# A decode step of attention and MLP layers: the last 64 outputs computed once, q spread by copies, and w4 in longer runs

## The chip, the core and the metric

The kernel runs on one core of one Trainium2 chip. The metric is the device time in microseconds of one execution; the time shown is the median of several runs. One further execution was recorded by the hardware profiler, and the page and the trace quoted here are of that one. PE is the matrix engine (PEld its weight loads), DVE the vector engine, ACT the scalar engine, POOL GpSimd, SP the engine whose queue issues the loads.

## What is computed

Eight sequences (B = 8) with one new token each, D = 448 features, go through an attention layer, an MLP layer, and both again with the same weights and the same K and V caches:

```python
x = A_x
x = x + A(layernorm(x))     # pass 0
x = x + B(layernorm(x))
x = x + A(layernorm(x))     # pass 1
x = x + B(layernorm(x))

def A(x):                   # 16 query heads, 8 K/V heads, 4096 cached keys, 256 wide
    q = x @ wq                                  # 448 -> 4096
    p = softmax(q . k_cache / 16)               # each K/V head serves two query heads
    return (p . v_cache) @ wo                   # 4096 -> 448

def B(x):                   # S = 1: the shifted branch through w1, w2 is zero
    x1 = x + 0
    return x1 + gelu(layernorm(x1) @ w3) @ w4   # 448 -> 1792 -> 448
```

With one token a sequence, each shifted part of B's first branch is padding, so w1 and w2 are not used. All inputs are bf16. A layer's caches are 268 MB, and pass 1 needs the same caches after pass 0, so nearly all of the traffic is K and V.

## The kernel before, in words

**Loads.** K and V come in pieces of 1 MB (two K/V heads, a quarter of the keys), each into one of 15 places in SBUF (`places`, L73). `emit_loads` (L616) issues them on SP's queue in the order of use, as soon as a place is free; eight DMA semaphores go round, so a load also waits for the one eight before it. Eleven pieces of each sequence stay in their places from pass 0 to pass 1, and a twelfth is parked in PSUM (`away`, L677) and brought back (`back`, L684). While they stay, few places are left to go round.

**Order.** `tasks` (L518) lists (pass, sequence, pair of K/V heads) by hand; each task has four K items and four V items, the V items one task later (L545). For a K item the vector engine transposes the place in two instructions (`transpose_k`, L640), PE multiplies by q (`scores`, L647), and after two items ACT takes the exponentials (L669). For a V item PE multiplies by the probabilities (`pv`, L708; in the last sequence `pv_cols`, L725). The place is then free, and the next load goes out.

**Chains.** What comes between attention and the next projection is written as generators: `first_half` and `chain` for pass 0 (wo, the MLP, the q of pass 1), `last` and `first_last` for pass 1, `rest` for the MLP of the first four sequences together. `step` (L768) lets each advance a little at each item, paced by the total number of its steps that `add_gen` is given. So their products stand between scores and PV products in PE's program, and their vector work between K transposes. The last MLP of the other four sequences runs at the end, after all loads (L899 onwards).

**The 448 features** are kept as columns: three groups of 128 partitions and one of 64 (`xT`, L169). In `wq` and `w3` the rows of the last 64 features are split over the partitions: half of the output columns in partitions 0 to 63, the other half in 64 to 127 (`split_tile`, `load_split`, L156 to L163). The input of those products, `xb`, therefore needs the last 64 features in the lower half for some products and the upper half for others (`wblk`, L174), with zeros in the other half. To have them in both, `xT` holds the last 64 features twice, and all that adds to xT makes them twice: `rows_to_cols` (L194) and `add_cols` (L332, five groups, of which fc 3 and fc 4 are the same 64 columns of the weights into the two halves). The weights of the mean, `wv` (L138), count each half by 0.5.

**Spreading q.** Scores need q in a block form `qbd` with zeros elsewhere. `spread_q` (L299) copies the selected rows of q to all four groups of 32 partitions by 16 products, and four `tensor_scalar` instructions with the 0/1 columns of `quad` write the whole of qbd. In pass 0 q comes from `qT1`, laid out with the eight sequences innermost, so one sequence's 32 columns are 16 bytes apart; in pass 1 from `qT2`, contiguous. Each (pass, sequence) is spread once (L807) into one of three buffers.

**w4** is loaded by L752 with hidden unit 128 c + p in partition p, block c: runs of 896 bytes. `mlp_hidden` (L352) makes the hidden units in the same order, 14 blocks of 128, each from 128 neighbouring columns of w3.

Of the kernel before, what the change touches and what calls it, by code (L numbers as in the profile page):

```python
# [17 lines left out]
def kernel(  # L18
# [39 lines left out]
    HC = F // 128  # L58
    scale_exp = float(Dh) ** -0.5
# [21 lines left out]
    def scratch(a, n):  # L81
# [8 lines left out]
    quad = consts.tile([128, 4], FP32, name="quad")  # L90
    nc.vector.tensor_reduce(
        quad[:], ident.rearrange("p (a j) -> p a j", a=4), mybir.AxisListType.X, ALU.add
    )


# [26 lines left out]
    for t in [sc] + o_banks:  # L122
        nc.vector.memset(t[:], 0.0)
# [14 lines left out]
    nc.vector.memset(wv[:, 3:4], 0.5 / D)  # L138
# [29 lines left out]
    w4_sb = consts.tile([128, HC, D], BF16, name="w4_sb")  # L168
    xT = consts.tile([128, 4, Bn], FP32, name="xT")  # L169
# [4 lines left out]
    def wblk(t, cols, c, fc):  # L174

        if fc < 3:
            return t[:, fc * cols + 128 * c : fc * cols + 128 * c + 128], fc
        half = cols // 2
        if 128 * c < half:
            return t[:, 3 * cols + 128 * c : 3 * cols + 128 * c + 128], 3  # L180
        return t[:, 3 * cols + 128 * c - half : 3 * cols + 128 * c - half + 128], 4

    def rows_to_cols(row, nb):

        idn = identb[:nb, :nb]
        ps = room_ps("y", nb)[:, 0 : 4 * nb].rearrange("p (f b) -> p f b", b=nb)
        for fc in range(3):  # L190
            nc.tensor.matmul(
                ps[:, fc, :], row[:nb, 128 * fc : 128 * fc + 128], idn, start=True, stop=True
            )
        for r in range(2):  # L194
            nc.tensor.matmul(
                ps[64 * r : 64 * r + 64, 3, :], row[:nb, 384:448], idn, start=True, stop=True
            )
        return ps

    def norm(x, nb, twice):  # L200
# [57 lines left out]
        parts = ((slice(0, 128), 0, 3, 0), (slice(0, 64), 3, 4, 3), (slice(64, 128), 3, 4, 4))  # L258
        for pp, f0, f1, to in parts:
            dst = xbs(nb)[pp, to : to + f1 - f0, :]  # L260
            if nb == 1:
                nc.vector.tensor_scalar(dst, xc[pp, f0:f1], rl[pp], c, ALU.mult, ALU.mult)  # L262
            else:
                nc.vector.scalar_tensor_tensor(
                    dst,
                    xc[pp, f0:f1],
                    c,
                    rl[pp].unsqueeze(1).to_broadcast([pp.stop - pp.start, f1 - f0, nb]),
                    ALU.mult,
                    ALU.mult,  # L270
                )
# [7 lines left out]
    def project_q(b0, nb, qT):  # L279
# [3 lines left out]
        for j in range(2):  # L283
            for h in range(Hq):
                for fc in range(4):
                    w, xi = wblk(wq_sb, HD, 2 * h + j, fc)
                    nc.tensor.matmul(  # L287
                        q_ps[:, j * Hq + h, :],
                        w,
                        xbs(nb)[:, xi, :],  # L290
                        start=(fc == 0),
                        stop=(fc == 3),
                    )
                if h % 4 == 3:
                    yield
# [3 lines left out]
    def spread_q(qT, qbd):  # L299


        qs = misc[:, 128 : 128 + 4 * NB2].rearrange("p (e n) -> p e n", e=4)
        for ep in range(4):
            e2, par = ep // 2, ep % 2
            sel = identb[:, 64 * e2 : 64 * e2 + 64].rearrange("p (j r) -> p r j", r=2)[:, par, :]
            for a in range(4):
                nc.tensor.matmul(  # L307
                    qs[32 * a : 32 * a + 32, ep, :], sel, qT, start=True, stop=True
                )
        yield  # L310
        for a in range(4):
            u = a // 2
            nc.vector.tensor_scalar_mul(  # L313
                qbd[:, :, :, a, :],
                qs.rearrange("p e (f g u h) -> p (e f) u g h", f=2, u=2, h=2)[:, :, u],
                quad[:, a : a + 1],
# [13 lines left out]
    def add_cols(y_ps, rhs, w, rows, every, open=None):  # L330

        for fc in range(5):  # L332
            lo, hi = (128 * fc, 128 * fc + 128) if fc < 3 else (384, 448)
            r = y_ps[:, fc, :] if fc < 3 else y_ps[64 * (fc - 3) : 64 * (fc - 2), 3, :]
# [14 lines left out]
            if fc % every == every - 1 or fc == 4:  # L349
                yield  # L350

    def mlp_hidden(b0, nb):  # L352
# [3 lines left out]
        for c in range(HC):  # L356
            for fc in range(4):
                w, xi = wblk(w3_sb, F, c, fc)
# [386 lines left out]
    nc.vector.tensor_copy(xT[:], ps0)  # L745
# [6 lines left out]
    nc.sync.dma_start(w4_sb[:], B_w4.rearrange("(c p) d -> p c d", p=128))  # L752
# [36 lines left out]
    for idx, it in enumerate(items):  # L789
        n, kv, c = it  # L790
        ps, b, gp = tasks[n]
        if (ps, b, gp, kv, c) == (0, Bn - 1, REST, 0, 0):
            assert pairs_done[1, MID - 1] == 4
            add_gen("rest", 0, rest(), idx + 1, idx + 18, 25)
# [4 lines left out]
        if kv == 0:  # L799
# [7 lines left out]
            if "q" not in st:  # L807
                qbd = work.tile([128, 8, GP, 4, 2], BF16, tag="qbd", bufs=3)
                run(spread_q(st["qT"][:] if ps == 1 else qT1[:, :, b], qbd))
                st["q"] = qbd  # L810
# [12 lines left out]
            if not paired(n, c):  # L823
                scores(p, c, st["q"], gp, between=turn)
            elif c % 2 != ps:
# [4 lines left out]
                if abs(two[1] - two[0]) == 1:  # L830
                    scores(two[0], x, st["q"], gp, also=two[1], between=turn)
                else:
                    scores(two[0], x, st["q"], gp, between=turn)
                    scores(two[1], x + 1, st["q"], gp)
# [8 lines left out]
        else:  # L843
# [6 lines left out]
            if final and gp in free:  # L850
                pv_cols(oc, slot, c, gp)
                if c % 2 == 1:
# [10 lines left out]
                            5,  # L863
# [14 lines left out]
            if c == 3:  # L878
                done = pairs_done[ps, b] = pairs_done.get((ps, b), 0) + 1
                if done == 2 and ps == 0:  # L880
                    add_gen("chain", b, first_half(b, st), idx + 1, idx + 21, 14)
                elif done == 2:
                    add_gen("chain" if final else "last", b, first_last(b, st), idx + 1, idx + 13, 11)
                elif done == 4 and ps == 0:
                    add_gen("chain", b, chain(b, st), idx + 1, first_of[(1, b), 0] - 1, 43)
# [15 lines left out]
    nc.vector.tensor_add(xs, xs, st["y"])  # L901
# [65 lines left out]
```

The softmax here doesn't subtract the row's maximum and nothing guards it: scores larger than these inputs give would overflow.

## Time and profile before

| | |
|---|---|
| median of 7 runs | 1119.17 us (1117.76 to 1121.62) |
| the profiled execution | 1116.47 us |
| its span | 1114.7 us |
| granted PE clock, mean | 0.586 of full speed |
| K loads, 1 MB each, median from issue to landing | 200, 11.6 us |
| V loads, 1 MB each, median from issue to landing | 216, 10.0 us |
| DVE K transposes (L645), two a load | 400, 469.0 us busy |
| PE scores (L660) | 7072 products, 268.0 us busy |
| PE PV products (L716) | 1984 products, 245.9 us busy |
| PE products with wo and w4, one sequence at a time, 64 wide (L341) | 512 and 224, 193 and 194 ns each |
| PEld weight loads of w3 (L359) | 560, 105 ns each |
| DVE writes of qbd (L313) | 64, 277 ns each |

The page divides the span into 40 slices. The busy digits are tenths, PEclk the clock that PE was granted in tenths, GB/s what the DMA engines moved:

```profile
PE   3135668657864688536894378944787478877866
...
DVE  5145554656365545555375553655537453585372
...
PEclk9999555755565555665555555555555555565575
DMA  9999999999999999999999999999999999999994
GB/s 357 383 421 421 412 395 417 419 407 416 405 422 421 404 405 421 418 422 381 398 420 421 421 390 399 418 421 410 398 400 421 417 403 413 419 380 412 405 419 175
```

A slice is 27.9 us. The rate is 412 to 422 GB/s in some, and 380 to 407 in others; the first two and the last one are lower still. In the groups of the page, busy time is the union of overlapping instructions, and the time of one matmul includes its way through the array, so products that follow each other start closer together than their duration says. Where spacings of starts are given below, they are read from the trace's instruction records, and sizes and durations of single DMA packets from its packet records.

### The profile page before, as it was taken

The numbers are of one execution on the slowest core, as the hardware profiler recorded it, in microseconds if no ns is written. First come the engines' busy times: TensorE is split into PE (matmuls) and PEld (weight loads), VectorE is DVE, ScalarE is ACT, GpSimd is POOL, SyncE is SP. The second block draws the span as 40 slices with busy tenths as digits, with TensorE's granted clock in tenths as the row PEclk, the third lists the DMA queues.
The fourth block names the chain that finished last, engine by engine and source line by source line (L and its number), as shares of the span: only waits on it lengthen the run. The fifth ranks groups of instructions, "written<-read, shape, count | busy, mean of one in ns | idle before, by whom it ended". The sixth has DMA issues, their size and how long they took to land.

```text
span 1114.7 us, 31093 instructions
## 1 busy us (share of the span) xinstructions
PE 734.9 (66%) x14193; PEld 459.4 (41%) x14193; DVE 595.2 (53%) x1040; ACT 135.9 (12%) x393; POOL 15.6 (1%) x25
## 2 busy tenths in 40 slices
PE   3135668657864688536894378944787478877866
PEld 2013445334541455214552145522554244645555
DVE  5145554656365545555375553655537453585372
ACT  0001101110110011101020011200111111111110
POOL 0000000000000000000000000000000000000000
PEclk9999555755565555665555555555555555565575
DMA  9999999999999999999999999999999999999994
GB/s 357 383 421 421 412 395 417 419 407 416 405 422 421 404 405 421 418 422 381 398 420 421 421 390 399 418 421 410 398 400 421 417 403 413 419 380 412 405 419 175
DMA packets 65170, 448.78 MB, mean 403 GB/s; under 512 B 6920, under 2 KB 10896, under 8 KB 11408
## 3 DMA queue, kind: packets, MB, share of 16 engines
q1 hardware_dynamic: 65008, 446.80, 98.3%
q8 instruction: 111, 1.82, 0.6%
q14 instruction: 19, 0.16, 0.0%
q10 hardware_dynamic: 32, 0.00, 0.0%
HBM read 446.77 MB, written 0.01 MB: 401 GB/s over the span
## 4 chain that ended last, share of the span: by engine, by line
DMA 59%; PE 20%; DVE 14%; SPq 3%; issue 2%; ACT 1%; POOL 0%; POOLq 0%; DVEq 0%; ACTq 0%
DMA places<-in_A_k_cache_dram 53%; DVE places L645 10%; PE sc L660 8%; DMA places<-in_A_v_cache_dram 5%; PE o L716 5%; PE misc L341 3%; PE misc L447 2%; SPq L161 2%; SPq L637 1%; DVE qbd L313 1%; DMA wq_sb<-in_A_wq_dram 1%; PE misc L287 1%; ACT p_n L669 0%; PE store L341 0%; PE store L730 0%
## 5 line engine op out<-in xcount | busy, mean ns | idle before, releaser
L645 DVE STREAM_TRANSPOSE places<-places 128x1024 uint32<-128x1024 uint32 x400 | 469.0, 1218 | 256.9 <-DMA places<-in_A_k_cache_dram 255.5
L660 PE MATMUL sc<-places,qbd 128*8 128x128 bf16 (+1 forms) x7072 | 268.0, 308 | 245.8 <-DVE places L645 215.4
L660 PEld LDWEIGHTS <-qbd 128*8 128x8 bf16 x7072 | 169.8, 107 | 347.3 <-issue 169.7
L716 PE MATMUL o<-places,ptw 128*16 128x512 bf16 x1984 | 245.9, 595 | 73.8 <-DMA places<-in_A_v_cache_dram 71.1
L669 ACT ACTIVATE p_n<-sc 128x256 bf16<-128x256 f32 x128 | 95.6, 747 | 738.2 <-PE sc L660 738.2
L341 PEld LDWEIGHTS <-wo_sb 128*128 128x128 bf16 (+1 forms) x1600 | 64.8, 125 | 43.4 <-issue 43.1
L716 PEld LDWEIGHTS <-ptw 128*16 128x16 bf16 x1984 | 44.2, 103 | 89.7 <-issue 80.9
L447 PEld LDWEIGHTS misc<-R,o_sb 128*128 128x128 f32 x248 | 54.6, 305 | 30.3 <-issue 19.5
L447 PE MATMUL misc<-R,o_sb 128*128 128x8 f32 x248 | 59.9, 352 | 10.6 <-ACT o_sb L442 4.9
L341 PE MATMUL misc<-OT,wo_sb 128*128 128x1 bf16 (+1 forms) x1280 | 56.7, 177 | 1.0 <-DVE qbd L313 1.0
L287 PEld LDWEIGHTS <-wq_sb 128*128 128x128 bf16 x1152 | 36.0, 104 | 45.6 <-issue 40.0
L287 PE MATMUL misc<-xb,wq_sb 128*128 128x1 bf16 x1024 | 34.7, 166 | 9.2 <-DVE xb L262 6.0
L669 ACT ACTIVATION_READ_ACCUMULATOR p_n<-sc 128x1 f32 x128 | 34.0, 266 | 0.0
L296 DVE CAST qT<-misc 128x32 bf16<-128x32 f32 x8 | 1.5, 191 | 59.5 <-PE misc L287 59.5
L703 ACT CAST ptw<-misc 128x128 bf16<-128x128 f32 x64 | 17.5, 274 | 128.0 <-PE misc L696 105.0
L442 ACT COPY o_sb<-o 128x256 f32<-128x256 f32 x62 | 23.5, 379 | 72.0 <-PE misc L447 63.8
L341 PEld LDWEIGHTS <-w_sb 128*128 128x128 bf16 (+1 forms) x630 | 25.9, 124 | 14.9 <-issue 14.8
L245 POOL TENSOR_TENSOR t<-t,nhalf 128x2 f32<-128x2 f32 (+2 forms) x18 | 13.3, 739 | 1085.4 <-DVE t L252 986.5
L313 DVE TENSOR_SCALAR qbd<-misc,quad 128x64 bf16<-128x64 f32 x64 | 13.7, 277 | 26.4 <-PE misc L307 26.4
L687 DVE STREAM_TRANSPOSE places<-store 128x512 uint32<-128x512 uint32 x32 | 20.1, 684 | 11.2 <-PE sc L660 11.2
L341 PE MATMUL misc<-HT_t,w_sb 128*128 128x1 bf16 (+1 forms) x560 | 25.2, 177 | 0.2 <-DVE HT_t L382 0.2
L359 PEld LDWEIGHTS <-w_sb 128*128 128x128 bf16 x560 | 18.0, 105 | 16.3 <-issue 16.0
(95 smaller groups left out, 267.8 us busy)
## 6 DMA issues: line engine op xcount, KB each, us to landing
places<-in_A_v_cache_dram SPq DMA_DIRECT2D x216, 1024.0 KB, 10.0
places<-in_A_k_cache_dram SPq DMA_DIRECT2D x200, 1024.0 KB, 11.6
wo_sb<-in_A_wo_dram SPq DMA_DIRECT2D x1, 3584.0 KB, 25.7
wq_sb<-in_A_wq_dram SPq DMA_DIRECT2D x3, 1024.0 KB, 7.0
w_sb<-in_B_w_dram SPq DMA_DIRECT2D x1, 1568.0 KB, 15.9
w_sb<-in_B_w_dram SPq DMA_DIRECT2D x3, 448.0 KB, 25.6
wq_sb<-in_A_wq_dram SPq DMA_DIRECT2D x2, 256.0 KB, 10.1
w_sb<-in_B_w_dram SPq DMA_DIRECT2D x2, 112.0 KB
```

The lines of the kernel that those rows point to most:

```text
L161: nc.sync.dma_start(t[:, fc * cols : (fc + 1) * cols], src[fc * 128 : fc * 128 + 128, :])
L287: nc.tensor.matmul(q_ps[:, j * Hq + h, :], w, xbs(nb)[:, xi, :], start=(fc == 0), stop=(fc == 3),)
L313: nc.vector.tensor_scalar_mul(qbd[:, :, :, a, :], qs.rearrange("p e (f g u h) -> p (e f) u g h", f=2, u=2, h=2)[:, :, u], quad[:, a : a + 1],)
L341: nc.tensor.matmul(r, w[:, i, lo:hi], rhs(i), start=start, stop=stop, skip_group_check=open is not None,)
L359: nc.tensor.matmul(h_ps[:, c * nb : c * nb + nb], w, xbs(nb)[:, xi, :], start=(fc == 0), stop=(fc == 3),)
L442: nc.scalar.copy(o_sb[:], o_ps[:, Dh * n : Dh * n + Dh])
L447: nc.tensor.matmul(ot_ps[:, n, j], o_sb[:].rearrange("p (i j) -> p j i", j=2)[:, j], R[:, n], start=True, stop=True,)
L645: nc.vector.transpose(w, w)
L660: nc.tensor.matmul(sc[32 * k : 32 * k + 8, 128 * x : 128 * (x + nx)], qbd[:, ep, gp].rearrange("p a h -> p (a h)"), v, start=(n == 0), sto ...
L669: nc.scalar.activation(p_sb[:, :, :, 2 * u : 2 * u + 2].rearrange("p t i x -> p x t i"), sc[:, 256 * u : 256 * u + 256].rearrange("p (x t ...
L687: nc.vector.transpose(slot[:].bitcast(U32)[:, 512 * n : 512 * n + 512], store[n][:].bitcast(U32))
L716: nc.tensor.matmul(o_ps[32 * q : 32 * q + 16, :].rearrange("p (i d) -> p i d", i=2), ptz[:, at : at + 16], rows[:, q, i : i + 2], start=(b ...
```

## The change

- **wo and w4, 64 outputs once.** `add_cols` has four groups instead of five; the fourth writes the last 64 features to partitions 0 to 63 only. `xT` keeps them there once, with zeros in the upper half; `rows_to_cols` makes them once, and `wv` has 1/D in the lower half and 0 in the upper. `norm` writes the upper copy in `xb` from the lower half of xc (an instruction whose input and output lie in different partitions). The misc bank is zeroed at the start.
- **q spread once.** `spread_q` makes four products instead of 16, into 32 partitions, and four copies that read these 32 partitions and write one group of 32 each. The zeros of qbd are written once at the start, so the buffers are two constants (`qbds`) instead of three rotating ones. When a (pass, sequence) is needed that is in neither, the one whose next use is farthest is replaced and spread again later: 18 spreads instead of 16. `quad` goes.
- **w4 in runs of 6,272 bytes.** Hidden unit 896 s + 7 p + c is in partition p, block 7 s + c. `mlp_hidden` makes its blocks in that order, so each takes every seventh column of w3 (`wblk` has a step). The products are the same in number and size.
- Totals given to `add_gen` follow the steps that went: 25 to 23, 14 to 13, 43 to 41.
- At the end, the addition to xT (L901) is in two instructions, of 128 and of 64 partitions, as is the first copy into xT.

The order of loads on SP is as before, but for the shape of w4's.

```diff
-    nc.vector.memset(wv[:, 3:4], 0.5 / D)
+    nc.vector.memset(wv[0:64, 3:4], 1.0 / D)
+    nc.vector.memset(wv[64:128, 3:4], 0.0)
...
+    qbds = [consts.tile([128, 8, GP, 4, 2], BF16, name=f"qbd{k}") for k in range(2)]
+    for t in qbds:
+        nc.vector.memset(t[:].rearrange("p n g a h -> p (n g a h)"), 0.0)
+    q_of = [None] * len(qbds)
...
-    def wblk(t, cols, c, fc):
+    def wblk(t, cols, at, step, fc):
...
+        s2 = at // half
+        lo = fc * cols + (at if fc < 3 else at - s2 * half)
+        return t[:, lo : lo + 127 * step + 1 : step], fc if fc < 3 else 3 + s2
...
-        qs = misc[:, 128 : 128 + 4 * NB2].rearrange("p (e n) -> p e n", e=4)
+        qs = misc[0:32, 128 : 128 + 4 * NB2].rearrange("p (e n) -> p e n", e=4)
         for ep in range(4):
...
-            for a in range(4):
-                nc.tensor.matmul(
-                    qs[32 * a : 32 * a + 32, ep, :], sel, qT, start=True, stop=True
-                )
+            nc.tensor.matmul(qs[:, ep, :], sel, qT, start=True, stop=True)
         yield
         for a in range(4):
             u = a // 2
-            nc.vector.tensor_scalar_mul(
-                qbd[:, :, :, a, :],
+            nc.vector.tensor_copy(
+                qbd[32 * a : 32 * a + 32, :, :, a, :],
                 qs.rearrange("p e (f g u h) -> p (e f) u g h", f=2, u=2, h=2)[:, :, u],
-                quad[:, a : a + 1],
             )
...
-        for fc in range(5):
-            lo, hi = (128 * fc, 128 * fc + 128) if fc < 3 else (384, 448)
-            r = y_ps[:, fc, :] if fc < 3 else y_ps[64 * (fc - 3) : 64 * (fc - 2), 3, :]
+        for fc in range(4):
+            lo, hi = 128 * fc, min(128 * fc + 128, D)
+            r = y_ps[0 : hi - lo, fc, :]
...
-                w, xi = wblk(w3_sb, F, c, fc)
+                w, xi = wblk(w3_sb, F, F // 2 * (c // H2) + c % H2, H2, fc)
...
-    nc.sync.dma_start(w4_sb[:], B_w4.rearrange("(c p) d -> p c d", p=128))
+    nc.sync.dma_start(
+        w4_sb[:].rearrange("p (s c) d -> p s (c d)", s=2),
+        B_w4.rearrange("(s p c) d -> p s (c d)", s=2, p=128),
+    )
...
-            if "q" not in st:
-                qbd = work.tile([128, 8, GP, 4, 2], BF16, tag="qbd", bufs=3)
-                run(spread_q(st["qT"][:] if ps == 1 else qT1[:, :, b], qbd))
-                st["q"] = qbd
+            if (ps, b) not in q_of:
+
+                def next_use(k):
+                    return next((m for m in range(n, len(tasks)) if tasks[m][:2] == q_of[k]), 999)
+
+                k = max(range(len(qbds)), key=next_use)
+                q_of[k] = (ps, b)
+                run(spread_q(st["qT"][:] if ps == 1 else qT1[:, :, b], qbds[k]))
+            qbd = qbds[q_of.index((ps, b))]
...
-    nc.vector.tensor_add(xs, xs, st["y"])
+    nc.vector.tensor_add(xs[:, 0:3], xs[:, 0:3], st["y"][:, 0:3])
+    nc.vector.tensor_add(xs[0:64, 3], xs[0:64, 3], st["y"][0:64, 3])
```

## The prediction

> **What bounds the kernel now.** I read the busy rows and queues of the page first, then the rate of the DMA over time, then, load by load from the trace, when each 1 MB load was issued and when it landed.
>
> ```profile
> PE 734.9 (66%) x14193; PEld 459.4 (41%) x14193; DVE 595.2 (53%) x1040; ACT 135.9 (12%) x393; POOL 15.6 (1%) x25
> ...
> q1 hardware_dynamic: 65008, 446.80, 98.3%
> q8 instruction: 111, 1.82, 0.6%
> ...
> DMA 59%; PE 20%; DVE 14%; SPq 3%; issue 2%; ACT 1%; POOL 0%; POOLq 0%; DVEq 0%; ACTq 0%
> ```
>
> The DMA engines hold packets 98.3% of the time and the chain of waits is mostly DMA. In full flow one load lands 2.48 us after another (423 GB/s); 446.8 MB at that pace is 1057 us, so 58 us of the 1114.7 us span are elsewhere. By 10 us windows held against 421 GB/s: 6.8 us before 50 us, about 25 us in dips between 130 and 1050 us, some 22 us at the end, mostly the 14 us after the last V load (1100.4 us).
>
> The dips matter most for a change to PE. They lie where the places not kept are few and two K and two V loads circulate. There a K transpose starts 0.02 us after its load lands almost every time: the engines wait for the DMA. A load lands either 2.48 us after the one before or, issued late, some 6.85 us after issue. I compared each landing with the later of those two. From 100 to 1062 us, 176 loads with an instruction packet (16,384 B) in flight came late by 29.4 us in all; 195 without one by 3.6 us. So the dips are mainly instruction fetches, each worth 0.27 us (29.4 / 111, which credits them with all of it). Late issue, which PE can cause, accounts for some 12 us and overlaps this.
>
> **The change, part by part.** All sums are against the profiled execution (1116.47 us: span 1114.7 plus 1.8); the median shown is 1119.17, 2.7 us more, and I put the difference on the median.
>
> **w4 in 6,272 B runs.** The load issued at L752 has 1,792 packets of 896 B and gets 256 of 6,272 B.
>
> ```profile
> GB/s 413 419 419 426 361 379 377 377 383 378 380 387 403 406 358 220 330 292 340 390 416 436 419 426 419 419 419 419 419 433 419 426 419 400 433 419 426 419 419 419
> ```
>
> This is the DMA rate from 20 to 70 us, 1.25 us a figure: 358, 220, 330, 292, 340 at 37.5 to 43.75 us is where w4 and the end of w3 pass. By packets: 1,792 x 51.8 ns / 16 engines is 5.8 us; between 3,584 B (150 ns) and 8,192 B (319 ns) a 6,272 B packet comes to 249 ns, and 256 of them to 4.0 us: 1.8 us gained. By landings: w4 came 4.45 us after the load before it, where 1.6 MB needs 3.8: 0.6 us gained. I take **-1.5**, nearer to the packets because the slow slices also hold the end of w3. A rule speaks against it: the Trainium skill, "DMA: Bandwidth & Descriptors", Specifications, puts full line rate at 512 B and more, which would make this 0. The trace has 17 B/ns for 896 B and 26 for 8,192 B, so the row decides. Nothing else hides or eats it: from 47 to 128 us every load lands on the 2.48 us pace, so all later landings move with it.
>
> **Fewer instructions.** PE's program falls from 27,768 to 26,508 rows; a fetch of 16,384 B holds 256 of 64 B, so 4.9 fewer fetches, at 0.27 us: **-1.3** (between 0 and that).
>
> **One 64-wide group instead of two.** `add_cols` had fc 3 and 4 of 64 columns each, the second a copy for the lower partitions.
>
> ```profile
> L341 PEld LDWEIGHTS <-wo_sb x32: 128/157/158, 518.0 to 519.4; 128*64 128x64 bf16 x32
> ...
>   DVE xT L479: 2.3, 1
> ```
>
> Those 32 loads start 48 ns apart, groups with one tile position 55 ns, while 128-wide ones start 27 ns apart. 446 go: 256 for wo one batch at a time, 112 for w4, 64 for wo with four columns, 14 for w4 with four: some 23 us of PE. Most of it lies beside DMA. It counts where the vector engine stands at L479 until the group is done, and the next K waits: the K transposes after these groups began 0.36, 0.62, 0.04, 0.38, 0.20, 0.61, 0.57 and 0.51 us after landing, 3.3 us in all. The group shrinks by 0.7 us, so this wait goes, but the load two later was late by only part of it: **-1.5** (0 to -3.3). What is late next is the K load itself.
>
> **w3 read at a step of 7.** This is the price of the w4 layout: hidden unit 7p + c belongs to partition p, so each of the 560 w3 weight loads at L359 takes columns 14 B apart.
>
> ```profile
> L359 PEld LDWEIGHTS <-w_sb x56: 103/104/114, 525.6 to 530.3; 128*128 128x128 bf16 x56
> ...
> L307 PE MATMUL misc<-qT,identb x16: 230/242/255, 503.7 to 503.9; 128*32 128x32 bf16 x16
> ...
> L307 PE MATMUL misc<-qT,identb x16: 187/188/235, 556.7 to 556.9; 128*32 128x32 bf16 x16
> ```
>
> The first row is contiguous; its loads start 26.7 ns apart. The other two are the same `spread_q` product: in pass 0 its 32 columns lie 16 B apart, in pass 1 2 B. Matmul ends are modelled, so I use starts: rounds of four tiles begin 51 to 59 ns apart in pass 0 and 27 in pass 1. Four streams that take a new 16 B line at each step run 2.1 times slower. The V products at L730 load weights at a 4 B step and keep 27 ns. Two rules meet here. The Trainium skill, "TensorE: Matmul & The Clock Gate", Weight-path perf modes, allows the fast load of 128 columns any step up to 1,024 elements: no cost. "SBUF — State Buffer", in its note on cachelines (16 B), wants two hits a line, yet calls 8 bf16 a free stride; the pass 0 row is exactly 8 and pays, while 14 B steps get 8 columns from 7 lines. I take the row: 27 to 56 ns, +29 ns a load. Lower bound 0; upper bound one line after another, 112 lines in 93 ns at the 0.83 ns pace of a fast load, or more.
>
> Where it lies: eight chains of 56 loads get +1.6 us each in steps of at most 16 or 24 loads (+0.5 to +0.7). Behind a step wait the PV products, whose V load is issued after them, and L377 on the vector engine with the next K. In the chain at 525 us, PE then idles 1.15 us for the K transpose and L377 ends 0.57 us before the next K lands, so most is covered: **+0.5** over the run. The `rest` stretch (950 to 995 us) has PE nearly full; 46 narrow loads go there (-2.4 us), 56 strided ones come (+1.6): **-0.5**.
>
> **Spreading q.** 16 products in four tile columns (about 0.14 to 0.20 us first to last start) become 4 in one, which no longer overlap: 4 x 27 or 4 x 56 ns, no gain. L313's four instructions of 277 ns (0.86 us) become four copies of 32 partitions and 64 columns; the nearest cast from PSUM is L296 at 191 ns for 32 columns, so 0.7 to 0.9 us: 0. The copies overwrite a buffer whose last scores stand before the products in PE's order, so two buffers for three add no wait. But 18 spreads replace 16: batch 2 of pass 0 and batch 5 of pass 1 are spread again, each about 1.2 us of PE and DVE in turn; the first falls in a PE stretch with the DMA at full rate, the second near 1000 us: **+0.5**.
>
> **Start.** Three more memsets (misc 0.49 us as its neighbours at L123, two of half L114's size) and a second xT copy lie before 12.6 us, while the q products wait for wq: 0. If exposed, below 1 us.
>
> **Tail.** DMA sets its start at 1100.4 us. What PE saves before (fc 4 of batch 7's wo, 0.9 us) is hidden by that V load; only the last group shrinks, 4 x 55 ns: -0.2. L901 becomes two: +0.16. Then
>
> ```profile
> 1107.21 1.65 PE misc L359 x56
> ```
>
> stands bare on the chain: 56 x 29 ns: +1.64. **+1.6** in all.
>
> **Pacing.** Generators lose one or two of their steps and totals fall with them; SP's order is the same but for w4. I count 0.
>
> **Sum:** -1.5 - 1.3 - 1.5 + 0.5 - 0.5 + 0.5 + 1.6 = **-2.2**, so 1114.3 against 1116.47, and 1119.17 - 2.2 = **1117.0**. What can be told from no change is 0.2%, 2.2 us: the forecast stands on that edge.
>
> **Rivals.** *A, slower: the strided load goes line by line.* At 93 ns a load is +66: tail +3.7 where the forecast has +1.6; each step of 16 or 24 becomes 1.1 to 1.6 us longer, past the 0.6 to 1.2 us of cover, about 1.3 us for each of eight chains (+10). With the gains kept: +9, **1128**, and far more if a line costs two steps. For it: four streams ask for 3.5 lines a step, L730 only one. Against: pass 0's spread asks for four lines a step and paid 2.1 times. It decides from about 70 ns a load. *B: no penalty.* Tail 0, middle -1.3 more: -5, **1114**. For it: L730 and the mode rule; against: the spread rows. *C: the middle hides everything.* The load behind each wait was late by little, and fetches may not be the cause: -1.5 + 0.5 + 0.5 + 1.6 = +1, **1120**.
>
> **How the numbers follow.** Forecast 0.54 (own range 1113 to 1121: faster 0.30, same 0.17, slower 0.07), A 0.26 (slower), B 0.13 (faster), C 0.07 (same 0.05, slower 0.02). Faster 0.43, same 0.22, slower 0.35. The range runs from 1112, below B, to 1129, A at 93 ns; beyond lies A at a heavier price.
>
> **What would show it.** Weight loads of the w3 line 53 to 60 ns apart and about 3.3 us for the 56 in the tail (1.65: B; over 5: A). w4 landing about 1.5 us earlier and the first loads after it too. Some 106 instruction packets of 16 KB. K transposes at once after landing where L479 had kept them. I am wrong if w3's steps move V issues or K transposes by a microsecond, or if the new order of steps sets other loads late.

## The result, and the profile after

The changed kernel takes **1129.69 us** (median of 12 runs, 1124.67 to 1135.46); the kernel before took 1119.18 beside it (30 runs). The ratio is 1.0087, with a 95% interval of 1.0070 to 1.0103: some 10 us slower, where 1117.0 was forecast. The granted PE clock is no cause: the eight executions at 0.58 to 0.59 of full speed took 1129.5 us in the mean, the four at 0.62 to 0.63 took 1128.7. The profiled execution took 1127.6 us, with a span of 1125.8, against 1116.47 and 1114.7.

The busy rows, the queues and the chain by engine, from the page of the changed kernel:

```profile
PE 722.8 (64%) x13562; PEld 450.2 (40%) x13562; DVE 600.3 (53%) x1054; ACT 136.5 (12%) x393; POOL 15.6 (1%) x25
...
q1 hardware_dynamic: 63472, 446.80, 97.7%
q8 instruction: 106, 1.74, 0.6%
...
DMA 59%; PE 22%; DVE 13%; issue 2%; SPq 2%; ACT 1%; POOL 1%; POOLq 0%; DVEq 0%; ACTq 0%
```

The change did what it said: 631 products fewer on PE, 106 instruction packets for 111, 1,536 packets fewer for w4. PE is busy 12 us less, and yet the kernel is slower: the DMA queue, the bound, now holds packets 97.7% of a longer span for 98.3%. The last V load lands at 1110.1 us for 1100.4, so 9.7 us of the loss arise before the tail.

The page's groups for the two operations that were priced, and three of the last lines of the chain of waits, long pieces only (start, us, what); in the groups the last columns are busy us, mean ns, and the idle time before with its releaser:

```profile
L303 DVE CAST qbd<-misc 32x64 bf16<-32x64 f32 x72 | 15.5, 215 | 52.3 <-PE misc L299 51.5
L348 PEld LDWEIGHTS <-w_sb 128*128 128x128 bf16 x560 | 33.3, 152 | 23.5 <-issue 23.3
```
```profile
1110.12 1.03 PE store L719 x32
1114.93 1.68 POOLq L962
1116.86 3.11 PE misc L348 x56
```

L348 is the old L359. Its loads take 152 ns for 105, and in the tail its 56 products take 3.11 us for 1.65. By the starts in the trace the loads there stand 53 to 54 ns apart for 27. The rate of the DMA over the same 20 to 70 us as before the change, 1.25 us a figure:

```profile
GB/s 413 419 426 416 367 375 387 377 378 376 386 393 401 410 359 273 363 376 427 432 418 419 419 419 419 419 426 433 419 419 419 426 400 426 419 419 419 433 419 419
```

The five slow figures from 37.5 us are now 359, 273, 363, 376, 427; w4 landed at 45.81 us for 47.03. All loads run 1.2 to 1.3 us ahead until 140 us. Then the lead is lost: the landings stand +1.7 us against before at 178 us, +3.9 at 548, +6.4 at 836, +10.2 at 1062. The loss comes mostly in steps, near the batches' MLPs; between them some of it is won back.

One such place, in the timeline (start, us, engine, line, operation, count, and in brackets the idle time before and who ended it), first of the kernel before:

```profile
540.13 0.91 PE L341 MATMUL misc<-HT_t,w_sb 128*64 128x1 bf16 x14
...
541.08 0.16 DVE L328 TENSOR_TENSOR xT<-xT,misc 128x4 f32<-128x4 f32 x1 [1.56 <-PE misc L341]
...
541.39 1.00 PE L447 MATMUL misc<-R,o_sb 128*128 128x8 f32 x4 [0.34 <-DVE xT L328]
...
542.10 2.37 DVE L645 STREAM_TRANSPOSE places<-places 128x1024 uint32<-128x1024 uint32 x2 [0.27 <-DMA places<-in_A_k_cache_dram]
...
542.31 1.03 PE L716 MATMUL o<-places,ptw 128*16 128x512 bf16 x8
...
543.27 0.59 PE L225 MATMUL misc<-t,one 128*128 128x2 f32 x2
```

and of the changed kernel:

```profile
539.48 0.91 PE L330 MATMUL misc<-HT_t,w_sb 128*64 128x1 bf16 x14
...
540.58 2.37 DVE L634 STREAM_TRANSPOSE places<-places 128x1024 uint32<-128x1024 uint32 x2 [3.18 <-DMA places<-in_A_k_cache_dram]
...
542.88 0.12 DVE L317 TENSOR_TENSOR xT<-xT,misc 128x4 f32<-128x4 f32 x1
...
543.15 0.99 PE L436 MATMUL misc<-R,o_sb 128*128 128x8 f32 x4 [2.75 <-DVE xT L317]
...
544.07 1.02 PE L649 MATMUL sc<-places,qbd 128*8 128x128 bf16 x32
...
545.02 0.59 PE L217 MATMUL misc<-t,one 128*128 128x2 f32 x2
...
545.65 0.16 DVE L220 COPY t<-misc 128x2 f32<-128x2 f32 x1 [2.06 <-PE misc L217]
...
546.88 1.03 PE L705 MATMUL o<-places,ptw 128*16 128x512 bf16 x8
...
546.98 0.58 DVE L255 TENSOR_SCALAR xb<-t 128x3 bf16<-128x3 f32 x3 [0.66 <-POOL t L237]
...
547.59 2.37 DVE L634 STREAM_TRANSPOSE places<-places 128x1024 uint32<-128x1024 uint32 x2
```

Before, the sum with w4 ends, the addition to xT (L328) follows at once, the half product (L447, which scales and transposes the PV result of half a finished sequence) and the PV product (L716) follow that, and the K transposes start as their load lands. After, the w4 sum is through at 540.4, but its addition (L317) stands behind a K load's two transposes in the vector engine's program and runs at 542.88. The half product (L436) waits 2.75 us for it, the scores (L649) stand behind that, the norm's product (L217, the layernorm's sums over partitions) behind the scores, and the vector engine waits for it at L220. Only after the whole norm does the vector engine come to the next K: its transposes start at 547.59, with no wait for DMA in their brackets. By the trace that load had landed 2.05 us earlier. The orders of the two built programs, in short (half: L447 and L436; norm: L225 and L217):

```
vector engine, before: K x2, L328, L217, L218, L220, K x2, L228 ... L252, L457, L458, L262
vector engine, after:  K x2, L317, L209, L210, L212, L220, L223, L233, L244, L255, K x2
PE, before: w4 x14, half, PV, norm, scores
PE, after:  w4 x14, half, scores, norm, half, PV
```

The waits of the whole run (us in total, times, longest) say that this is no single case. Before:

```profile
DVE t L228 <- PE misc L225: 2.1, 3, 0.7
...
PE misc L447 <- DVE xT L328: 1.7, 5, 0.3
```

After:

```profile
DVE t L220 <- PE misc L217: 13.1, 9, 2.1
PE misc L436 <- DVE xT L317: 12.3, 5, 2.8
```

The half product's wait comes five times, once for each batch whose chain meets a half of a finished sequence (PE's order has it behind five of the eight w4 sums). Read from the trace, the K load behind the norm waited at these five places for 0.02 us each before, and for 1.64, 2.05, 1.91, 1.87 and 2.12 us after: 9.6 us. A sixth place is like them in effect: in batch 0's MLP, near 150 us, two K loads in a row wait 3.25 and 2.34 us, for 0.62 and 0.03 before.

What late transposes do to the DMA can be estimated with the forecast's own rule, that a load lands 2.48 us after the one before or 6.85 us after its issue. Where the second is the later, the load was issued too late to keep the queue full. From 100 us to 38 us before the last V load this late issue sums to 8.2 us before (the forecast had some 12) and 27.0 after; 16 us of the 27 lie near the six places, where it was 1.

### The profile page after: what moved, and what is told of

Read it like the earlier page. It is cut to its first block, busy times and chain, and to the rows that moved or that the text cites. A ratio compares the mean times of both kernels' runs of the same rounds, so it can differ in the third digit from the quotient of the medians.

```text
span 1125.8 us, 29840 instructions
## 1 busy us (share of the span) xinstructions
PE 722.8 (64%) x13562; PEld 450.2 (40%) x13562; DVE 600.3 (53%) x1054; ACT 136.5 (12%) x393; POOL 15.6 (1%) x25
## 3 DMA queue, kind: packets, MB, share of 16 engines
q1 hardware_dynamic: 63472, 446.80, 97.7%
## 4 chain that ended last, share of the span: by engine, by line
DMA 59%; PE 22%; DVE 13%; issue 2%; SPq 2%; ACT 1%; POOL 1%; POOLq 0%; DVEq 0%; ACTq 0%
DMA places<-in_A_k_cache_dram 48%; DVE places L634 10%; DMA places<-in_A_v_cache_dram 9%; PE sc L649 8%; PE o L705 5%; PE misc L436 3%; PE misc L348 2%; SPq L157 2%; PE misc L330 2%; DVE qbd L303 1%; DMA w_sb<-in_B_w_dram 1%; DMA wq_sb<-in_A_wq_dram 1%; POOL t L237 1%; PE misc L280 1%; PE misc L403 0%
## 5 line engine op out<-in xcount | busy, mean ns | idle before, releaser
L649 PE MATMUL sc<-places,qbd 128*8 128x128 bf16 (+1 forms) x7072 | 268.8, 307 | 242.8 <-DVE places L634 213.8
L649 PEld LDWEIGHTS <-qbd 128*8 128x8 bf16 x7072 | 170.2, 107 | 344.9 <-issue 173.8
L436 PE MATMUL misc<-R,o_sb 128*128 128x8 f32 x248 | 59.8, 351 | 21.7 <-DVE xT L317 12.3
L436 PEld LDWEIGHTS misc<-R,o_sb 128*128 128x128 f32 x248 | 54.7, 305 | 47.2 <-issue 36.2
L330 PEld LDWEIGHTS <-wo_sb 128*128 128x128 bf16 (+1 forms) x1280 | 47.6, 114 | 31.4 <-issue 31.0
L280 PEld LDWEIGHTS <-wq_sb 128*128 128x128 bf16 x1152 | 35.6, 105 | 39.9 <-issue 38.2
L303 DVE CAST qbd<-misc 32x64 bf16<-32x64 f32 x72 | 15.5, 215 | 52.3 <-PE misc L299 51.5
L348 PEld LDWEIGHTS <-w_sb 128*128 128x128 bf16 x560 | 33.3, 152 | 23.5 <-issue 23.3
L330 PE MATMUL misc<-OT,wo_sb 128*128 128x1 bf16 (+1 forms) x1024 | 41.7, 171 | 0.9 <-ACT ptw L692 0.8
L348 PE MATMUL misc<-xb,w_sb 128*128 128x1 bf16 (+1 forms) x560 | 34.1, 192 | 12.6 <-DVE xb L255 7.4
L280 PE MATMUL misc<-xb,wq_sb 128*128 128x1 bf16 x1024 | 34.6, 166 | 4.4 <-ACT ptw L692 3.3
L403 PE MATMUL misc<-zm,one 128*128 128x8 f32 (+1 forms) x66 | 18.0, 346 | 13.7 <-DVE zm L395 6.6
L330 PEld LDWEIGHTS <-w_sb 128*128 128x128 bf16 (+1 forms) x504 | 19.0, 117 | 17.8 <-issue 17.7
```

The costliest lines, as they stand in the source:

```text
L280: nc.tensor.matmul(q_ps[:, j * Hq + h, :], w, xbs(nb)[:, xi, :], start=(fc == 0), stop=(fc == 3),)
L303: nc.vector.tensor_copy(qbd[32 * a : 32 * a + 32, :, :, a, :], qs.rearrange("p e (f g u h) -> p (e f) u g h", f=2, u=2, h=2)[:, :, u],)
L330: nc.tensor.matmul(r, w[:, i, lo:hi], rhs(i), start=start, stop=stop, skip_group_check=open is not None,)
L348: nc.tensor.matmul(h_ps[:, c * nb : c * nb + nb], w, xbs(nb)[:, xi, :], start=(fc == 0), stop=(fc == 3),)
L436: nc.tensor.matmul(ot_ps[:, n, j], o_sb[:].rearrange("p (i j) -> p j i", j=2)[:, j], R[:, n], start=True, stop=True,)
L649: nc.tensor.matmul(sc[32 * k : 32 * k + 8, 128 * x : 128 * (x + nx)], qbd[:, ep, gp].rearrange("p a h -> p (a h)"), v, start=(n == 0), sto ...
```

## The experiments

Each kernel ran beside the kernel before on the same chip; ratios are to that, with 95% intervals. A submission is a set of kernels that ran together in this way. First the parts were undone one by one.

**e1_steps: the changed kernel with the lost steps back.**

```diff
             if fc % every == every - 1 or fc == 3:
                 yield
+        if every < 4:
+            yield
...
-                    add_gen("chain", b, chain(b, st), idx + 1, first_of[(1, b), 0] - 1, 41)
+                    add_gen("chain", b, chain(b, st), idx + 1, first_of[(1, b), 0] - 1, 43)
```

(The other two totals go back in the same way, 23 to 25 and 13 to 14.)

> The changed kernel with an empty fifth step after each four-group wo or w4 sum and the totals 25, 14, 43 of before, so that every step falls at the item where it fell before. Theory P (pacing: with one or two steps fewer, the xT addition after w4 falls behind two K transposes and holds PE and a V load): the middle comes back, about 1119 us (start -1.2, tail +1.5, little else), and PE's wait for that addition falls from 12.3 us to about 2. Theory S (the strided w3 loads delay V loads and K transposes): unchanged, 1128 to 1130.

1118.23 us, ratio 0.9989 (0.9972 to 1.0006). An empty step takes 11 us off the changed kernel: the half product's wait for the addition is gone from its list of waits, the late K transposes at the five places are gone too (0.02 us each), and L220's wait is as short as before:

```profile
DVE t L220 <- PE misc L217: 2.1, 3, 0.7
```

**e2_layout: the changed kernel with w4 in 896 B runs and w3 by neighbouring columns.**

```diff
-                w, xi = wblk(w3_sb, F, F // 2 * (c // H2) + c % H2, H2, fc)
+                w, xi = wblk(w3_sb, F, 128 * c, 1, fc)
...
-        w4_sb[:].rearrange("p (s c) d -> p s (c d)", s=2),
-        B_w4.rearrange("(s p c) d -> p s (c d)", s=2, p=128),
+        w4_sb[:],
+        B_w4.rearrange("(c p) d -> p c d", p=128),
```

> The changed kernel with w4 in 896 B runs and w3 columns taken next to each other, as before; all else as changed. S: 1119 to 1121, the middle comes back with the 27 ns loads. P: 1129 to 1130, since 1.2 us are lost at the start and 1.5 gained in the tail, and the middle stays.

1123.24 us, ratio 1.0025 (1.0007 to 1.0043). So the layout isn't free either: without it 6.5 us less. The five late K loads are still there (1.7 to 2.1 us each).

**e3_both: both undone**, which leaves the 64 outputs computed once and q spread by four products.

> Both undone: old steps and old layout, so what is left is wo and w4 once and q spread once. P: 1117 to 1119, as the first of these runs less the tail plus the start. S: 1117 to 1119 too, as the second. If it stays above 1124, neither is the cause and it lies in the spreading of q or in the narrow groups.

1113.36 us, ratio 0.9948 (0.9925 to 0.9970): faster than both kernels.

**e4_merge: the kernel before, with nothing but the steps of fc 3 and fc 4 taken together.**

```diff
-            if fc % every == every - 1 or fc == 4:
+            if (fc != 3 and fc % every == every - 1) or fc == 4:
```

The totals 25, 14 and 43 become 23, 13 and 41.

> The kernel before with its fourth and fifth group of wo and w4 in one step and the totals 23, 13, 41 of the change, nothing else. P: 1127 to 1131, the loss of the change without any of its other parts. S: 1118 to 1120, no change.

1126.61 us, ratio 1.0060 (1.0032 to 1.0087), with not one operation changed. It has the two waits:

```profile
DVE t L228 <- PE misc L225: 13.0, 9, 2.1
...
PE misc L447 <- DVE xT L328: 10.6, 5, 2.7
```

At the five places its K loads wait 2.04, 2.07, 2.07, 2.00 and 2.05 us. So the pacing costs by itself; 1127 to 1131 was expected of it, and 1126.61 is just below that.

**e5_stride and e6_runs: the layout's two halves apart**, each from e3_both; e5 has only w3's step of 7, e6 only w4's long runs.

> This is the changed kernel with its pacing as before (the empty step) and with w4 in 896 B runs again, while w3 is still read at a step of 7; the hidden units then meet the wrong rows of w4, so the output is of another MLP, with the same products in number and size. Against the version with both parts undone (0.9948 of before): theory 'the strided reads of w3 cost the middle' expects +6 us, +1.5 of it in the tail, so 1119 to 1121 and a ratio of 1.000 to 1.002. Theory 'only the long w4 packets and the shifted start disturb the middle' expects the tail's +1.5 alone: 1115, ratio 0.996.

> This is the changed kernel with its pacing as before and with w4 in 6,272 B runs, while w3 is read by neighbouring columns; the output is again of another MLP, with the same products in number and size. Theory 'the strided reads of w3 cost the middle' expects the start's gain alone against the version with both parts undone: -1.2 us, so 1112, ratio 0.9937. Theory 'the earlier start moves the loads into a worse place against the rest' expects the middle's loss here: 1117 to 1118, ratio 0.999.

e5: 1118.32 us, 0.9993 (0.9974 to 1.0012). e6: 1112.34 us, 0.9947 (0.9926 to 0.9967). What the layout costs comes from the strided read; the long runs cost nothing that can be told. Their gain at the start is smaller than the 1.2 us by which w4 landed earlier: w4 lands at 45.7 to 45.8 us in the four traces with long runs and at 46.1 to 47.0 in eleven that have short runs and some or all of the other edits (e8 left out; means 45.73 and 46.44). That is 0.7 us, too little to tell in the total.

**e7_narrow: the kernel before with the 64 outputs once, and nothing else of the change**; q is spread in the old way (16 products, `quad`, three buffers).

> This is the kernel before with the 64 outputs computed once, its pacing, its w4 and w3 and its way of spreading q (16 products, three buffers) kept. The version with both parts undone, which spreads q by four products as well, took 0.9948 of before (-6 us). Theory 'the narrow groups bring it all' (forecast: -1.5 for the groups and most of -1.3 for fetches, both too small) expects 1113 to 1114 here, ratio 0.995. Theory 'spreading q brings it' (fewer instructions between two batches and shorter vector work, 215 ns for 277) expects 1117 or more, ratio 0.998 or more.

1113.94 us, 0.9951 (0.9934 to 0.9967): the gain is the narrow groups'; spreading q makes no difference that can be told.

**e8_step: the strided read by itself.**

```diff
-                w, xi = wblk(w3_sb, F, 128 * c, 1, fc)
+                w, xi = wblk(w3_sb, F, F // 2 * (c // H2), c % H2 + 1, fc)
```

> This measures the disputed read by itself: w3's columns are taken at a step of 1, 2, 3, 4, 5, 6 and 7 for the blocks c = 0 to 6 and again for c = 7 to 13 (so not all hidden units are made, and some twice; the products are the same in number and size; pacing and w4 as before). Spacing of the starts of the weight loads in the last MLP, by step. Theory 'the array reads four columns at a time and takes a new 16 B line at each' expects 27 ns at a step of 1 and 2 (two or more columns a line), and some 53 ns from 5 on (one a line), with 3 and 4 between or at 27. Theory 'any step but 1 loses the fast read' expects 53 ns or more at step 2 already. Theory 'bytes spanned set it' expects a rise in proportion to the step.

In the last MLP the starts of successive loads, read from the trace, stood apart by:

| step, columns of 2 B | 1 | 2 | 3 | 4 | 5 | 6 | 7 |
|---|---|---|---|---|---|---|---|
| ns from start to start | 27 | 27 | 27 to 30 | 32 to 34 | 39 to 40 | 46 to 47 | 53 to 55 |
| bytes from first to last column | 256 | 510 | 764 | 1,018 | 1,272 | 1,526 | 1,780 |

A step of 2 is free, and 3 nearly so. From 4 on the time goes with the bytes spanned, 31 to 33 B/ns, above a floor of 27 ns: the third theory, with a floor, and not a jump at the step where each column has a line of its own. With no step above 7, e8 can't tell bytes spanned from 16 B lines touched: up to a step of 8 (16 B) every line in the span is touched.

**e9_chains and e10_wide: the step of 7 only in the eight single-sequence chains, or only in the two MLPs of four sequences**, from e3_both. The edit of e9; e10 has `nb > 1` in its place:

```diff
-                w, xi = wblk(w3_sb, F, 128 * c, 1, fc)
+                at, step = (F // 2 * (c // H2) + c % H2, H2) if nb == 1 else (128 * c, 1)
+                w, xi = wblk(w3_sb, F, at, step, fc)
```

> Where does the strided read of w3 cost its 5 us? The version with both parts undone, with w3 read at a step of 7 only in the eight chains of one sequence each; the two MLPs of four sequences read neighbouring columns (so the single-sequence MLPs pair their hidden units with other rows of w4; products the same in number and size). Theory 'the chains': each of eight chains gets 1.5 us longer, in front of PV products and the V places they free; then most of the middle's 3.5 us is here: 1116.5, ratio 0.997 to 0.9985, against 0.9948 without any stride. Theory 'the forecast's cover holds, and the four-sequence MLPs carry the cost': 1113.5, ratio 0.9950.

> The other half: a step of 7 only in the two MLPs of four sequences (the one in the stretch after 950 us, and the bare one at the end), the chains with neighbouring columns (the hidden units of those two MLPs then meet other rows of w4; products the same in number and size). Theory 'the chains' expects the tail's +1.5 and little more than 0 from the stretch: 1115, ratio 0.996 to 0.9965. Theory 'the four-sequence MLPs carry the cost' expects 1118, ratio 0.999.

e9: 1115.90 us, 0.9976 (0.9960 to 0.9992). e10: 1118.41 us, 0.9989 (0.9971 to 1.0008). Together they make more than the whole (e5), and in e10's profile the loads fall 2.9 us behind e3's by 587 us, where the two programs are the same. That casts doubt on differences of this size.

**e14_none, e15_tail, e16_rest: e3_both once more, then the step of 7 only in the last MLP, then only in the stretch after 950 us** (conditions `b0 > 0 and nb > 1` and `b0 == 0 and nb > 1`).

> The version with both parts undone once more, as the base for the next two on the same chip. If one submission is like another, 0.9948 again (0.993 to 0.997). If versions built alike differ by 2 to 3 us between submissions, 0.997 or more, and the split of the stride's cost can't be told by differences of that size.

> The same with w3 at a step of 7 only in the last MLP, which stands bare behind all loads (its hidden units meet other rows of w4; products the same in number and size). 56 loads at 53 ns for 27: +1.5 us by the forecast's own price, so a ratio 0.0013 above the base run beside it, 0.996 to 0.9965; the middle has no edit, so anything more than +1.5 is not the stride's.

> The same with the step of 7 only in the four-sequence MLP of the stretch after 950 us (its hidden units meet other rows of w4; products the same in number and size). Theory 'the stretch carries the cost' expects +3 us over the base run beside it: ratio 0.9975. The forecast's own reckoning has +1.6 us of PE there, beside DMA: between 0 and +1.6, ratio 0.9948 to 0.9962.

e14: 1115.48 us, 0.9979 (0.9961 to 0.9997). e15: 1116.67 us, 0.9988 (0.9971 to 1.0006). e16: 1114.45 us, 0.9965 (0.9951 to 0.9979). The same kernel gave 0.9948 and 0.9979, 3.5 us apart. The tail's step is clear in the chain of waits (1.65 us for 56 products in e14, 3.11 in e15), but no single part of the middle can be read from differences of 1 to 3 us between submissions. What can be told, roughly, is the mean of several: four runs with no strided read and the old pacing (e3, e14, e6, e7) have 0.9956, the two with all of it (e1, e5) 0.9991, so the step of 7 costs about 0.0035, 3.9 us. Within one submission the difference is 0.0041 (e1 and e3) and 0.0042 to 0.0046 (e5 and e7, e6), 4.6 to 5.1 us. Where it is paid the traces show better than the times: late issue, reckoned as above from one trace of each, is 9.9 to 11.6 us in the three runs with the strided read in the chains (e1, e5, e9) and 4.3 to 8.1 in the seven without (e3, e6, e7, e10, e14, e15, e16).

**e11_w4 and e13_add: which wait makes the pacing cost.** e11 is e3_both without the empty step behind the w4 sum alone (first edit; totals 24, 14 and 42). e13 has no empty steps in `add_cols`, but one behind w4's addition to xT (second edit; totals 23, 13 and 42):

```diff
-        if every < 4:
+        if every < 4 and w is wo_sb:
             yield
...
         nc.vector.tensor_add(xs, xs, y_ps)
+        if nb == 1:
+            yield
```

> Which of two waits makes the pacing cost? The version with both parts undone, without the empty step behind the w4 sum (totals 42 and 24); wo's sums keep theirs. In the order of PE's program the norm's product now stands before the half product and the PV product, right behind a K item's scores, and the vector engine's copy of its result follows with no K transposes between; but the half product still stands in the item before the addition to xT. Theory a, 'the half product that waits for the xT addition behind K transposes' (12 us of waits after, 1.7 before), expects that wait gone and the time as without the merge: 1113 to 1114, ratio 0.995. Theory b, 'the vector engine waits for the norm's product behind scores, with the next K transposes behind it' (13 us in 9 waits after, not among the long ones before), expects the wait of 2.1 us nine times here and a loss of 5 us or more: 1119 or more, ratio 1.000 or more.

> Both waits together, without any change of layout: the version with both parts undone, with wo's and w4's empty steps taken out (totals 23, 13 and 42) and one empty step put behind w4's addition to xT in the chains. By the order of PE's program the half product should stand behind the xT addition, and the norm's product before the PV product, as in the changed kernel. Both theories expect the loss of the merged pacing: 1119 to 1124, ratio 1.000 to 1.004. If it is as fast as without the merge (0.995), neither of the two waits is the cause, and the place of other steps is.

e11: 1115.32 us, 0.9960 (0.9943 to 0.9977). e13: 1120.37 us, 1.0014 (0.9997 to 1.0031). Both have the norm's product ahead of the PV product, and the vector engine takes the norm's result before the next K transposes. Their waits, e11 first:

```profile
DVE t L220 <- PE misc L438: 7.7, 5, 1.5
...
DVE t L220 <- PE misc L217: 3.4, 5, 0.7
```
```profile
DVE t L220 <- PE misc L438: 14.6, 5, 2.9
...
PE misc L438 <- DVE xT L317: 10.3, 5, 2.7
...
DVE t L220 <- PE misc L217: 3.5, 5, 0.8
```

L438 is their half product. In e11 it doesn't wait for the addition, the norm comes through sooner, and K waits 0.02 to 0.26 us at the five places; in e13 it waits, and K waits 1.04 to 1.61 us, 6.8 us in all, beside the 0.0054 (6 us) between the two. Theory b's order without long waits is as good as free. They also differ in wo's steps, so this is strong, not clean, evidence for theory a.

**e17_swap and e18_swap_before: only the wait of the half product taken away**, in the changed kernel and, as a control, in the kernel before.

```diff
-        for kind in ("chain", "last", "rest"):
+        for kind in ("last", "chain", "rest"):
```

> The changed kernel, layout and all, with one line other: at each item the generator of the finished sequence's half (kind last) advances ahead of the chain's. The half product then stands ahead of the addition to xT and doesn't wait for it; the vector engine's order is unchanged around that addition, and the norm's product still stands in front of the PV product. Theory a, 'the half product that waits for the xT addition behind K transposes': its wait of 12.3 us in 5 is gone and the time falls from 1.0087 to 1.000 to 1.003 (1119 to 1122). Theory b, 'the norm's product in front of PV and behind the scores': no gain, 1.007 or more.

> The kernel before with the same swap, as the control: its half product waited only 1.7 us in 5 for that addition, so both theories expect no change, 0.998 to 1.002. A gain of 5 us here would say that the swap helps by something else.

e17: 1133.93 us, 1.0138 (1.0109 to 1.0167). e18: 1117.19 us, 0.9995 (0.9975 to 1.0015). Theory a's number is missed: the swap made it worse. The list of waits of e17 shows what came instead:

```profile
PE misc L280 <- DVE qT L447: 18.6, 5, 3.7
PE misc L330 <- DVE rz L406: 13.1, 5, 2.6
...
DVE t L220 <- PE misc L436: 7.8, 5, 1.6
```

The wait for the addition is gone, but the first product with w4 (L330) now waits as long, in five places again, for a reciprocal (L406) that stands behind another K load's transposes in the vector engine's program, with that load's scores behind L330. The wait moved 4 to 5 us ahead and did not go. A longer one is new: the first product with wq (L280) waits for the half's result (L447), which stands behind the next K load's transposes, and that load's scores stand behind L280 (near 548 us PE is idle for 3.73 us). The changed kernel has no such wait. So this run doesn't tell theory a from b. The control shows that in the kernel before the swap changes nothing that can be told, and one thing more: its K loads wait 0.44 to 0.58 us at the five places, at no cost in time that can be told.

## Why the prediction was wrong, step by step

| step | forecast, us | what the runs showed |
|---|---|---|
| w4 in longer runs | -1.5 | -0.7 by the landings; in the total not to be told (e6) |
| narrow groups, fetches, q, last group | -1.5 - 1.3 + 0.5 - 0.2 | -4.9, the mean of e3, e14, e6, e7 (-2.4 to -5.9) |
| w3 at a step of 7, tail | +1.64 | +1.46 (3.11 for 1.65) |
| the same, middle | +0.5 - 0.5 | some +2.4 to +3.7 (3.9 to 5.1 less the tail) |
| pacing | 0 | +6 to +11 |

**The step that failed is the pacing**: "Generators lose one or two of their steps and totals fall with them; SP's order is the same but for w4. I count 0." SP's order is the same indeed, but the orders of PE's and the vector engine's programs are not. A step less puts the w4 sum one item earlier against the K items, so its addition falls behind a K load's transposes, and a half product, scores, norm and the next K stand in a row behind it. The cost was measured four ways: 0.0060 in the kernel before (e4, 6.7 us), 0.0069 and 0.0058 for e2 and e13 against the 0.9956 without stride, and 0.0096 for the changed kernel against e1 and e5: 6 to 11 us. That the merged steps cause it is shown by e1 and e4, which change no operation. That the time is lost through late K loads is read in the traces, not shown by an edit: at the five places e2, e4, e13 and the changed kernel have 6.8 to 10.2 us of it, the kernel before, e1 and e11 0.1 to 0.9; e17, whose waits sit elsewhere, has 4.1 there and 3.6 at the K loads two before, and e18 2.7 without a loss. Late issue divides them in the same way: 16.8 to 29.6 us in the five runs with a loss (the changed kernel, e2, e4, e13, e17), 4.3 to 13.6 in all others. Which one of the waits in that row is the first cause was not isolated.

**A term was mis-sized: w3's middle.** The price a load was right (56 ns forecast, 53 measured), from the row of pass 0's spreading and not from the rule of the Trainium skill that allows the step ("TensorE: Matmul & The Clock Gate", Weight-path perf modes); so was the tail. The cover was overrated. In e1 the K transposes at 535, 668 and 1029 us, where the hidden units of a chain are made, start 0.51, 0.48 and 0.45 us late, in e3 0.02; in batch 0 two in a row start 1.33 and 1.35 us late, in e3 0.98 and 0.03. That these are the cost is likely, by the late issue in e1, e5 and e9, but not shown: e18's waits of half a microsecond cost nothing that can be told. The reason given, a new 16 B line at each column, is not what e8 shows: steps of 4 to 6 already pay, in proportion to the bytes spanned, though at those steps two or more columns share some lines.

**w4's longer runs were oversized.** The forecast had 1.8 us by packets and 0.6 by landings and took 1.5; 0.7 came. The 6,272 B packets took 284 ns in the mean, for 249 forecast.

**Undersized on the other side: the narrow groups.** With the fetches, q and the last group they were thought good for 2.5 us, and brought about 5. The waits behind L479 went as forecast: the next K load after each of the eight groups waits 0.02 us in e3, for 2.5 us in all before (the forecast's 3.3 takes in two K loads further on, of 0.62 and 0.20 us). Why more was gained was not isolated. Spreading q came out at nothing to be told (e3 and e7), as costed; its copies take 215 ns each, between the forecast's 191 and the old 277. The 106 instruction packets are as forecast; what a fetch is worth could not be read by itself.

Together: -4.9 + 3.9 + 9.6 (the five late K loads, in full) = +8.6, beside the measured 0.0087 x 1119 = +9.7. This is a rough sum: in e4 10.2 us of late K loads cost 6.7 us, and batch 0's are not in it.

Rival A stood at 1128, close to the result, with another mechanism: 93 ns a load, deciding from 70. The loads stand 53 ns apart, so A is false, and its time was met by accident. B is false as well. C is false too: the gains did come through (e3, e7), and the loss in the middle was not in it. The last sentence of the prediction had named what happened, loads set late by the new order of steps, without giving it a price.

## What to carry to other kernels

When work is spread over a loop by counting steps, taking one instruction group out is also a change of the order of everything behind it: lay the built orders of PE and the vector engine beside each other before counting it at nothing, and look for what now stands between a landed load and the instruction that uses it. Here a late use kept a place busy, the next load was issued late, and the bound, the DMA queue, ran short. Keep an empty step in the place of a removed one first; that version (e3, e14) beats the kernel before, and the layout of w4 is better left as it was, since a step of 7 costs the weight loads of w3 more than the longer runs bring. Repeat the base version before reading differences of 0.3% between submissions: here the same kernel gave 0.9948 and 0.9979.

## What the runs showed of the hardware

- Weight loads of 128 columns with a step between them keep 27 ns at a step of 2 elements (4 B), 27 to 30 at 6 B, and then slow down steadily, 32 to 34 ns at 8 B and 53 to 55 at 14 B: 31 to 33 bytes spanned a nanosecond (e8, steps of 1 to 7).
- A K load that waits half a microsecond for its transposes costs nothing that can be told (e18: five times 0.44 to 0.58 us, ratio 0.9995, 0.9975 to 1.0015), while of 2 us in five places some two thirds came into the total (e4: 10.2 us of waiting, 6.7 us of time).
